# Loading four of sixteen input chunks of a Fourier stage by three wide transfers in place of eight narrower ones

## The chip, the cores and the metric

One core of one Trainium2 chip runs the whole program. The metric is device time in microseconds (us) of one execution, less is better. The kernel before took 1183.57 us, the median of three runs (1179.47 to 1185.5).

## What is computed

The input x has 2 batches of 3008 positions and 256 features. The reference is a Fourier layer followed by two wide two-layer networks:

```python
X = np.fft.rfft(x, axis=1)
Yr = Xr @ w_r - Xi @ w_i + b_r
Yi = Xr @ w_i + Xi @ w_r + b_i
Yr, Yi = shrink(Yr, 0.01), shrink(Yi, 0.01)   # sign(v) * max(|v| - lam, 0)
x = irfft(Y, n=3008)                          # 6016 rows of 256
h = x @ w_in;  x = (h * cos(h)) @ w_out       # 256 -> 2048 -> 256
h = x @ w_in2; x = (h * clip(h + 3, 0, 6) / 6) @ w_out2
```

## The kernel before, in words

The discrete Fourier transform over 3008 = 47 x 64 positions is cut in two. The first half, called part a here, multiplies slices of x by a table of sines and cosines ("ta"). Its work is listed in `a_list`: sixteen chunks, numbered 0 to 15, chunks 0 to 7 for batch 0 and 8 to 15 for batch 1. A chunk covers 4 of the 32 position pairs. Its x slice is 96 rows (partitions) of 4 pairs x 256 features x 4 bytes = 4 KB, 384 KB in all; its table slice is 96 rows of 4 x 96 x 4 bytes = 1.5 KB, 144 KB in all. Together a chunk is 528 KB.

`load_x` (line 494) issues a chunk's two transfers on SP's queue, the table first (line 504), then x (line 508; chunk 0's x goes in two pieces). Chunks 0 to 2 and 7 to 15 go through tiles "ta" and "x" with three buffers each. Chunks 3 to 6 have a place of their own, `x_big` (line 483): one persistent tile of 96 rows, in which each chunk has a stretch with 4 KB of x and then 1.5 KB of table. In HBM a row of x holds 32 KB for one batch, a row of the table 12 KB, so a chunk's rows are pieces of longer rows.

`a_part` (line 511) does half a chunk: four matrix products into one PSUM bank (line 515), a copy by ACT (line 524) and, for batch 0, a subtraction by DVE (line 526). In the loop of lines 718 to 729 the engine PE takes chunks 0 to 7 in order, two `a_part` calls each, and one dummy product (line 723, tile "wp") after each half. Nothing else is there for PE to do at that time. Only when chunk 7 is done can the next stage begin: `w_mm` (line 588, tile "pp") reads what all eight chunks wrote to zh and zl. Chunks 8 to 15 are then done one per step between the products of that stage.

The order on SP's queue is the order in which the code issues. Chunks 0 to 6 are issued ahead of everything (line 533), then the weights w_r and w_i of the layer (tile "wst", 256 KB each, lines 552 and 553), then chunk 7, the tables of the next stage (fg_raw, bias_raw), chunk 8 and so on. SP's transfers are counted on eight counters in turn (DMAHW0 to DMAHW7 in the rows of the order below), and a transfer that takes up a counter again first waits until the transfer eight before it has landed.

PE, SP and ACT run in the order in which the code is written here.

Of the kernel before, what the change touches and what calls it, by code (L numbers as in the profile page):

```python
# [9 lines left out]
F32 = mybir.dt.float32  # L10
# [11 lines left out]
NB, D, DFF = 2, 256, 2048  # L22
# [5 lines left out]
ROWS = 2 * DOF  # L28
# [22 lines left out]
XB, NBIG = 3, 4  # L51
# [73 lines left out]
def fourier_moe_moe_kernel(ctx, tc, x, w_r, w_i, b_r, b_i, ta, tg, fg, win1, wout1, win2, wout2, out):  # L125
    nc = tc.nc
    pe, act, dve, sp = nc.tensor, nc.scalar, nc.vector, nc.sync
# [4 lines left out]
    persist = ctx.enter_context(tc.tile_pool(name="persist", bufs=1))  # L132
# [343 lines left out]
    with ExitStack() as actx:  # L476
        apool = actx.enter_context(tc.tile_pool(name="apool", bufs=1))
        with tc.manual_schedule(engines={mybir.EngineType.PE, mybir.EngineType.SP, mybir.EngineType.Activation}):
# [1 line left out]
            zh = apool.tile([128, NP, 2, 4, N2], F32R, name="zh")  # L480
            zl = apool.tile([128, NP, 2, 4, N2], F32R, name="zl")

            x_big = persist.tile([ROWS, NBIG, 4 * (ROWS + D)], F32, tag="zt", name="x_big")
            z1 = None
            x_t, ta_t = {}, {}
            a_list = []
            for b in range(NB):
                p0 = 0
# [5 lines left out]
            def load_x(a):  # L494
                if a >= len(a_list):
                    return
                b, p0, n = a_list[a]
                if XB <= a < XB + NBIG:
                    tt = x_big[:, a - XB, 4 * D :]
                    xt = x_big[:, a - XB, : 4 * D].rearrange("p (n e) -> p n e", e=D)  # L500
                else:
                    tt = apool.tile([ROWS, 4 * ROWS], F32, tag="ta", bufs=XB, name=f"ta{a}")
                    xt = apool.tile([ROWS, 4, D], F32, tag="x", bufs=XB, name=f"x{a}")
                sp.dma_start(tt[:, : n * ROWS], ta[:, p0 * ROWS : (p0 + n) * ROWS])
                parts = 2 if a == 0 else 1
                for k in range(parts):
                    i0, i1 = k * n // parts, (k + 1) * n // parts
                    sp.dma_start(xt[:, i0:i1], x[b, :, p0 + i0 : p0 + i1, :])
                x_t[a], ta_t[a] = xt, tt
# [23 lines left out]
            for a in range(XB + NBIG):  # L533
                load_x(a)
# [131 lines left out]
            def k2_step(i):  # L666
# [28 lines left out]
                if a < 2 * NA:  # L695
                    a_part(a, 1)
                    load_x(a + XB)
# [20 lines left out]
            for c in range(NA):  # L718
                for kc in range(2):
                    if c == NA - 1:  # L720
                        constants(kc)
                    a_part(c, kc)
                    pe.matmul(wp, lhsT=warm[:, 0, 0:128], rhs=warm, start=True, stop=True)
                if c < XB:
                    load_x(XB + NBIG + c)
                if c == 0:
                    late_loads2()
                elif c == XB:
                    late_loads3()
# [27 lines left out]
    with tc.manual_schedule(engines=engines):  # L757
# [39 lines left out]
        def bank(z, name):  # L797
            return psum.tile([128, 512], F32, tag=f"h{z}", bufs=1, name=name)
# [123 lines left out]
        for k in range(2 * G):  # L922
            n = HALF[k // STEPS % NJ]
            a, b, c, d = (bank(z, f"h{r}_{k}") for z, r in zip((0, 1, 2, 3) if k % 2 == 0 else (0, 3, 2, 1), "abcd"))
# [125 lines left out]
```

## Time and profile before

| what | value |
|---|---|
| median of three runs | 1183.57 us (1179.47 to 1185.5) |
| the profiled execution's own time | 1183.19 us |
| its span (first to last instruction) | 1181.4 us |
| mean granted TensorE clock over the span | 0.998 |
| PE busy | 1157.2 us, 98% of the span |
| POOL, ACT, DVE busy | 67%, 69%, 64% |
| DMA | 101.98 MB, mean 86 GB/s |

PE has work almost all of the time, so a delay of PE early in the program is a delay of the end unless PE would have waited later anyway. The stage that the change touches lies in the first 30 us of the span. Times in the rows below count from the span's start. In the rows "SPq" is the transfer queue of SP; a row of it stands for the issue of a transfer, not for its landing.

### The profile page before, as it was taken

The page shows a single profiled execution, that of the slowest core. Times are in us where ns is not written, and L with a number is a line of the kernel's source. Part 1 is how long each engine was busy: PE and PEld are TensorE (multiplying, and loading weights), DVE is VectorE, ACT ScalarE, POOL GpSimd, SP SyncE. Part 2 cuts the span into 40 slices and gives each one's busy share as a digit, 9 for nine tenths or more (in the row PEclk, how much of TensorE's full clock was granted, in tenths as well). Part 3 has the DMA queues.
Part 4 walks back from the last instruction along what each step waited for, and adds up shares of the span by engine and source line. Part 5 has one row for each costly group of instructions (what it writes and reads, how often), then busy time and mean ns, then how long its engine had stood idle before and what let it go on. Part 6 is the DMA issues. An engine that isn't in the chain of part 4 may idle for free.

```text
span 1181.4 us, 15880 instructions
## 1 busy us (share of the span) xinstructions
PE 1157.2 (98%) x5379; PEld 967.7 (82%) x5379; DVE 760.5 (64%) x1090; ACT 812.1 (69%) x1542; POOL 795.8 (67%) x633
## 2 busy tenths in 40 slices
PE   8999898999999999999999999999999999999998
PEld 6888776778888888888888988888888888888897
DVE  3787768887679888898897677643343444433442
ACT  3677667777788888888888876665565556555554
POOL 0456455797778797888886886556757667667544
PEclk9999999999999999999999999999999999999999
DMA  9646647644431313103114520020020010100000
GB/s 229 173 124 181 200 150 249 231 118 128 134 109 57 90 60 116 54 19 132 52 36 152 197 103 1 1 72 1 1 72 1 12 61 1 60 8 1 36 1 32
DMA packets 49354, 101.98 MB, mean 86 GB/s; under 512 B 6164, under 2 KB 23832, under 8 KB 48632
## 3 DMA queue, kind: packets, MB, share of 16 engines
q1 hardware_dynamic: 49272, 100.97, 27.1%
q8 instruction: 42, 0.69, 0.3%
q14 instruction: 40, 0.33, 0.1%
HBM read 61.76 MB, written 39.19 MB: 85 GB/s over the span
## 4 chain that ended last, share of the span: by engine, by line
PE 88%; DMA 4%; DVE 3%; ACT 2%; POOL 1%; issue 1%; SPq 1%; POOLq 0%; DVEq 0%; ACTq 0%
PE acc L802 41%; PE hb L802 15%; PE ha L802 10%; PE hc L802 5%; PE hd L802 5%; PE pp L588 4%; PE yp L390 2%; PE bp L615 2%; PE zp L515 1%; DMA tg_sb<-in_tg_dram 1%; PE vp L654 1%; POOL gl L174 1%; DMA x_big<-in_x_dram 1%; DMA x<-in_x_dram 1%; DMA st<-x_dram 1%
## 5 line engine op out<-in xcount | busy, mean ns | idle before, releaser
L174 POOL TENSOR_TENSOR gl<-r,gh 128x512 fp32r<-128x512 f32 (+1 forms) x384 | 501.5, 1321 | 283.8 <-ACT gh L793 264.0
L802 PE MATMUL acc<-gh,wo 128*128 128x512 f32 (+1 forms) x1536 | 529.7, 386 | 0.0
L802 PEld LDWEIGHTS acc<-gh,wo 128*128 128x128 f32 x1536 | 288.4, 188 | 53.5
L802 PE MATMUL acc<-gl,wo 128*128 128x512 f32 (+1 forms) x768 | 295.9, 385 | 0.6 <-POOL gl L174 0.6
L802 PE MATMUL hb<-tok,wi 128*128 128x512 f32 (+1 forms) x864 | 241.0, 387 | 0.6 <-DVE hc L814 0.6
L793 ACT ACTIVATE gh<-r 128x512 fp32r<-128x512 f32 (+1 forms) x384 | 227.5, 615 | 0.4 <-PE acc L802 0.4
L802 PEld LDWEIGHTS hb<-tok,wi 128*128 128x128 f32 x864 | 160.9, 188 | 31.5 <-DVE hc L814 2.4
L814 DVE TENSOR_TENSOR hd<-p,hb 128x512 f32<-128x512 f32 (+1 forms) x96 | 65.7, 684 | 163.0 <-PE hb L802 157.9
L802 PEld LDWEIGHTS acc<-gl,wo 128*128 128x128 f32 x768 | 144.2, 188 | 27.6 <-POOL gl L174 1.0
L786 ACT ACTIVATE r<-r 128x512 f32<-128x512 f32 (+1 forms) x192 | 118.8, 619 | 62.5 <-DVE r L778 62.5
L802 PE MATMUL ha<-tok,wi 128*128 128x512 f32 (+1 forms) x576 | 160.2, 386 | 0.4 <-ACT yo L400 0.4
L802 PEld LDWEIGHTS ha<-tok,wi 128*128 128x128 f32 x576 | 107.8, 188 | 21.6 <-ACT yo L400 1.7
L439 POOL TENSOR_TENSOR tok<-st,tok 128x512 fp32r<-128x512 f32 (+1 forms) x77 | 97.6, 1282 | 4.1 <-ACT tok L436 4.1
L943 ACT ACTIVATE p<-hc 128x512 f32<-128x512 f32 (+1 forms) x96 | 56.6, 589 | 57.9 <-PE hc L802 57.8
L780 ACT ACTIVATE r<-hd 128x512 f32<-128x512 f32 (+1 forms) x48 | 28.3, 589 | 78.4 <-PE hd L802 78.4
L934 ACT ACTIVATE hb<-ha 128x512 f32<-128x512 f32 (+1 forms) x96 | 55.2, 575 | 38.5 <-PE ha L802 38.5
L802 PE MATMUL hc<-tok,wi 128*128 128x512 f32 (+1 forms) x288 | 80.2, 387 | 1.2 <-DVE r L787 1.1
L802 PE MATMUL hd<-tok,wi 128*128 128x512 f32 (+1 forms) x288 | 79.7, 385 | 0.0
L814 DVE TENSOR_TENSOR hc<-p,hb 128x512 f32<-128x512 f32 (+1 forms) x96 | 65.4, 681 | 15.2 <-PE hb L802 14.4
L802 PEld LDWEIGHTS hc<-tok,wi 128*128 128x128 f32 x288 | 53.7, 188 | 12.5 <-DVE r L787 2.6
L802 PEld LDWEIGHTS hd<-tok,wi 128*128 128x128 f32 x288 | 54.1, 188 | 10.1
L177 POOL TENSOR_TENSOR w<-cvai,cvbi 128x512 f32<-128x512 f32 x16 | 20.9, 1306 | 57.0 <-DVE cvbi L216 57.0
(134 smaller groups left out, 1709.0 us busy)
## 6 DMA issues: line engine op xcount, KB each, us to landing
st<-x_dram SPq DMA_DIRECT2D x20, 512.0 KB, 5.1
wi<-wi_dram SPq DMA_DIRECT2D x5, 1792.0 KB, 8.0
rawi<-in_win_dram SPq DMA_DIRECT2D x16, 512.0 KB, 4.2
rawo<-in_wout_dram SPq DMA_DIRECT2D x16, 512.0 KB, 4.0
u_dram<-v SPq DMA_DIRECT2D x48, 128.0 KB, 2.4
u_sb<-u_dram SPq DMA_DIRECT2D x16, 384.0 KB, 4.1
wo<-wo_dram SPq DMA_DIRECT2D x10, 512.0 KB, 7.6
x_dram<-o SPq DMA_DIRECT2D x20, 256.0 KB, 2.3
```

The lines of the kernel that those rows point to most:

```text
L174: nc.gpsimd.tensor_tensor(out, x, y, op=ALU.subtract)
L390: pe.matmul(yp[:, i * TP : (i + 1) * TP], lhsT=u_sb[g][:, i, ec * 128 : (ec + 1) * 128], rhs=tg_sb[g][:, i * TP : (i + 1) * TP], start=Tru ...
L439: subtract(at(lo, t), src, f32(at(hi, t)), op=ALU.subtract)
L588: pe.matmul(pp.rearrange("p a e -> p (a e)"), lhsT=za[:, p, kc, 2 * (k2 % 2) : 2 * (k2 % 2) + 2, :].rearrange("p r n -> p (r n)"), rhs=wb[ ...
L615: pe.matmul(bp, lhsT=fgr[:, fi, :], rhs=src[:, :, m, :], start=(n == 0 and not by_pe), stop=(n == 5))
L780: act.activation(r, h, AF.Relu, bias=3.0, scale=1.0)
L786: act.activation(r, r, AF.Sin, bias=math.pi / 2, scale=1.0)
L793: act.activation(gh[:, :n], self.r[:, :n], AF.Copy)
L802: pe.matmul(h[:, :n], lhsT=w, rhs=x, start=start and j == 0, stop=stop and j == 2, skip_group_check=True)
L814: dve.tensor_tensor(h[:, :n], r[:, :n], x[:, :n], op=ALU.add)
L934: act.activation(b[:, :n], a[:, :n], AF.Copy)
L943: act.activation(p5[:, :n], c[:, :n], AF.Copy)
```

## The change

The transfers of chunks 3 to 6 are replaced. The buffer `x_big` keeps its size and place, but is laid out as one stretch with the x of all four chunks (16 KB per row) and behind it the table of all four (6 KB per row). One transfer brings the whole table (96 rows of 6 KB, 576 KB), and two bring x, for two chunks each (96 rows of 8 KB, 768 KB). Chunks 3 to 6 read their pieces out of it.

```diff
-            x_big = persist.tile([ROWS, NBIG, 4 * (ROWS + D)], F32, tag="zt", name="x_big")
+            x_big = persist.tile([ROWS, NBIG * 4 * (ROWS + D)], F32, tag="zt", name="x_big")
+            big_x = x_big[:, : NBIG * 4 * D].rearrange("p (n e) -> p n e", e=D)
+            big_t = x_big[:, NBIG * 4 * D :]
...
                 if XB <= a < XB + NBIG:
-                    tt = x_big[:, a - XB, 4 * D :]
-                    xt = x_big[:, a - XB, : 4 * D].rearrange("p (n e) -> p n e", e=D)
+                    z = 4 * (a - XB)
+                    x_t[a], ta_t[a] = big_x[:, z : z + 4], big_t[:, z * ROWS : (z + 4) * ROWS]
+                    if z == 0:
+                        sp.dma_start(big_t, ta[:, p0 * ROWS : (p0 + 4 * NBIG) * ROWS])
+                    if z % 8 == 0:
+                        sp.dma_start(big_x[:, z : z + 8], x[b, :, p0 : p0 + 8, :])
+                    return
```

No instruction of PE, ACT, DVE or POOL is added, removed or moved. On SP's queue, before, chunks 3 to 6 and what follows (ta and x are the tiles of a chunk, the last number in a name counts buffers; the square brackets name the counters that the transfer waits for):

```order
L504 DMA x_big_108<-in_ta_dram 96x384
L508 DMA x_big_108<-in_x_dram 96x1024 [waits DMAHW0_49]
L504 DMA x_big_108<-in_ta_dram 96x384 [waits DMAHW1_49]
L508 DMA x_big_108<-in_x_dram 96x1024 [waits DMAHW2_49]
L504 DMA x_big_108<-in_ta_dram 96x384 [waits DMAHW3_49]
L508 DMA x_big_108<-in_x_dram 96x1024 [waits DMAHW4_49]
L504 DMA x_big_108<-in_ta_dram 96x384 [waits DMAHW5_49]
L508 DMA x_big_108<-in_x_dram 96x1024 [waits DMAHW6_49]
L552 DMA wst_148<-in_w_r_dram 128x2x256 [waits DMAHW7_49]
L553 DMA wst_148<-in_w_i_dram 128x2x256 [waits DMAHW0_49]
L504 DMA ta7_170<-in_ta_dram 96x384 [waits DMAHW1_49,PE_49]
L508 DMA x7_171<-in_x_dram 96x1024 [waits DMAHW2_49]
```

The same place in the changed kernel, whose line numbers are up to seven higher:

```order
L504 DMA x_big_108<-in_ta_dram 96x1536
L506 DMA x_big_108<-in_x_dram 96x2048 [waits DMAHW0_49]
L506 DMA x_big_108<-in_x_dram 96x2048 [waits DMAHW1_49]
L559 DMA wst_143<-in_w_r_dram 128x2x256 [waits DMAHW2_49]
L560 DMA wst_143<-in_w_i_dram 128x2x256 [waits DMAHW3_49]
L511 DMA ta7_165<-in_ta_dram 96x384 [waits DMAHW4_49,PE_49]
L515 DMA x7_166<-in_x_dram 96x1024 [waits DMAHW5_49]
```

Eight rows have become three, each of more bytes; the order of the rest is as it was, and each still waits for the transfer eight before it.

On PE, before, chunk 3 and the first product of chunk 4 (zp is the PSUM bank that they write, "warm" the dummy product's operand, x3 three more products alike):

```order
L515 MATMUL zp_0_219<-x_big 128x96 [waits DMAHW7_49,DMAHW0_49,DVE_49]
L515 MATMUL zp_0_219<-x_big 128x96 x3
L723 LDWEIGHTS warm
L723 MATMUL wp<-warm 128x512
L515 MATMUL zp_1_227<-x_big 128x96 [waits DVE_49]
L515 MATMUL zp_1_227<-x_big 128x96 x3
L723 LDWEIGHTS warm
L723 MATMUL wp<-warm 128x512
L515 MATMUL zp_0_243<-x_big 128x96 [waits DMAHW2_49,DMAHW1_49,DVE_49]
```

and in the changed kernel the end of chunk 3, chunk 4 and the first product of chunk 5:

```order
L522 MATMUL zp_1_222<-x_big 128x96 [waits DVE_49]
L522 MATMUL zp_1_222<-x_big 128x96 x3
L730 LDWEIGHTS warm
L730 MATMUL wp<-warm 128x512
L522 MATMUL zp_0_238<-x_big 128x96 [waits DVE_49]
L522 MATMUL zp_0_238<-x_big 128x96 x3
L730 LDWEIGHTS warm
L730 MATMUL wp<-warm 128x512
L522 MATMUL zp_1_246<-x_big 128x96 [waits DVE_49]
L522 MATMUL zp_1_246<-x_big 128x96 x3
L730 LDWEIGHTS warm
L730 MATMUL wp<-warm 128x512
```

The first product of chunk 4 (zp_0_238) has lost its wait for two transfers. Chunk 3's first product, ahead of these rows, still waits for two (DMAHW7 and DMAHW0), which are now the whole table and the x of two chunks; chunk 5's, behind them, waits for the second x transfer (DMAHW1).

## Rows read from the trace of the kernel before

**Rows 1.** The page: busy time of each engine.
```profile
PE 1157.2 (98%) x5379; PEld 967.7 (82%) x5379; DVE 760.5 (64%) x1090; ACT 812.1 (69%) x1542; POOL 795.8 (67%) x633
```
**Rows 2.** Chain of waits, 0 to 30 us: start us, us, what.
```profile
5.41 9.55 DMA x_big<-in_x_dram
...
14.97 8.98 DMA x<-in_x_dram
...
24.09 1.10 PE zp L515 x8
```
**Rows 3.** What PE waited for: total us, times, longest us.
```profile
PE zp L515 <- DMA x<-in_x_dram: 3.1, 2, 2.0
```
**Rows 4.** Timeline of PE: start us, us, engine line, tile [idle before].
```profile
8.30 1.10 PE L515 MATMUL zp<-ta,x 96*128 96x96 f32 x8 [1.11 <-DMA x<-in_x_dram]
...
12.59 0.38 PE L723 MATMUL wp<-warm 128*128 128x512 bf16 x1
12.80 1.10 PE L515 MATMUL zp<-x_big 96*128 96x96 f32 x8
13.74 0.38 PE L723 MATMUL wp<-warm 128*128 128x512 bf16 x1
13.96 1.03 PE L515 MATMUL zp<-x_big 96*128 96x96 f32 x8
...
19.72 1.10 PE L515 MATMUL zp<-x_big 96*128 96x96 f32 x8
...
24.09 1.10 PE L515 MATMUL zp<-ta,x 96*128 96x96 f32 x8 [1.96 <-DMA x<-in_x_dram]
...
25.30 1.86 PE L515 MATMUL zp<-ta,x 96*128 96x96 f32 x8
...
27.02 0.99 PE L588 MATMUL pp<-wh,zh 128*128 128x512 f32 x1
...
29.34 1.03 PE L515 MATMUL zp<-ta,x 96*128 96x96 f32 x8
30.15 0.48 PE L588 MATMUL pp<-wh,zh 128*128 128x512 f32 x1
...
31.62 1.03 PE L515 MATMUL zp<-ta,x 96*128 96x96 f32 x8
```
**Rows 5.** Timeline of SP: issues, each released by the landing eight before it.
```profile
8.18 0.31 SPq L508 DMA_DIRECT2D x_big<-in_x_dram  x1
...
10.44 0.31 SPq L508 DMA_DIRECT2D x_big<-in_x_dram  x1
...
12.72 0.39 SPq L553 DMA_DIRECT2D wst<-in_w_i_dram  x1
...
19.60 0.22 SPq L558 DMA_DIRECT2D bias_raw<-in_b_r_dram  x1
...
24.02 0.31 SPq L504 DMA_DIRECT2D ta<-in_ta_dram  x1
```
**Rows 6.** Stretches: busy us by engine, granted clock, DMA share, GB/s.
```profile
6.00:22.00 16.00, 14.89 (x118) 13.09 (x116) 7.25 (x13) 6.35 (x14) 0.00 (x0) 1.00 1.06 242
7.00:8.00 1.00, 0.19 (x1) 0.00 (x0) 0.47 (x2) 0.49 (x1) 0.00 (x0) 1.00 1.02 244
8.00:9.00 1.00, 0.70 (x6) 0.73 (x7) 0.09 (x1) 0.00 (x0) 0.00 (x0) 1.00 1.05 233
25.20:28.50 3.30, 3.30 (x13) 2.93 (x13) 1.99 (x4) 1.50 (x3) 0.00 (x0) 0.50 0.84 224
18.00:19.00 1.00, 1.00 (x11) 0.97 (x10) 0.40 (x1) 0.49 (x1) 0.00 (x0) 1.00 1.08 210
213.00:216.00 3.00, 3.00 (x15) 2.49 (x14) 2.96 (x3) 0.82 (x2) 2.67 (x2) 1.00 0.98 401
```
**Rows 7.** Transfers of the first 60 us by line: count, KB each, us to landing.
```profile
x_big<-in_x_dram SPq DMA_DIRECT2D x4, 384.0 KB, 8.9
```

## The prediction

> **What bounds the kernel now.** I read the page first: PE is busy 98% of the span [rows 1], so what counts is whatever makes PE idle or slow. The list of what PE waited for comes next. Of the waits for input, one line concerns the stage of the change: part a's products waited 3.1 us in all, twice, for an x transfer [rows 3]. The timeline of PE shows where: 1.11 us before chunk 1 (at 8.30) and 1.96 us before chunk 7 (at 24.09) [rows 4]. Between them chunks 1 to 6 follow each other without a wait; from the start of chunk 3 (12.80) to that of chunk 6 (19.72) a chunk takes (19.72 - 12.80) / 3 = 2.31 us [rows 4].
>
> The chain of waits says what stands behind chunk 7: two transfers, 9.55 and 8.98 us from issue to landing, fill the time from 5.41 to 23.95 [rows 2]; the four x transfers of chunks 3 to 6 take 8.9 in the median [rows 7]. These are long because they stand in line. The stretch from 6 to 22 us has a DMA share of 1.06 at 242 GB/s [rows 6]: all 16 engines always have something to move, and bytes set the pace. The timeline of SP gives the landings, since each issue there is released by the landing of the transfer eight before it: x of chunk 1 lands at 8.18, of chunk 2 at 10.44, of chunk 3 at 12.72, of chunk 6 at 19.60, of chunk 7 at 24.02 [rows 5]. Five chunks in 19.60 - 8.18 = 11.42 us is 2.28 us for a chunk's 528 KB. So data come at almost the rate at which PE uses them, chunk by chunk, and chunk 3 starts 0.08 us after its data are there.
>
> One more thing hangs on the last wait. [...] From chunk 7's start to the first product behind the six of line 588 it takes 29.34 - 24.09 = 5.25 us; at full clock a chunk takes 2.31 and the next such six, from 30.15 to 31.62, take 1.47 [rows 4], 3.78 together. The fall thus costs about 1.47 us. The 1.11 us of idleness before chunk 1 were not followed by a fall: the clock stays at 1.00 in the two stretches around it [rows 6].
>
> **The change part by part.** *Issues.* SP issues five transfers fewer, worth 0.31 us of its time each at the pace seen there [rows 5]. That is nothing for the sum: SP is waiting for landings anyway, and the engines behind it are never without work [rows 6].
>
> *Bytes.* They are the same, in the same places of the line up to chunk 2 and from wst on. If the rate holds, chunk 7 lands at 24.02 as before, and so does all that follows.
>
> *The rate.* No row of before shows 96 rows of 6 or 8 KB. The nearest row, and the one I take, is the same tensors in the same line at 242 GB/s (2.28 us per 528 KB). The upper end is 401 GB/s, in the stretch 213 to 216 us, which moves a weight tile of 128 rows of 14 KB; the lower is the slowest stretch in this line, 210 GB/s at 18 to 19 us [rows 6]. The first is far from this case in shape and source, so it stays an end. [...]
>
> *What chunk 3 waits for.* This is the cost. It needs the whole table (576 KB) and the x of two chunks (768 KB), 1344 KB behind chunk 2 instead of 528. At 2.28 us per 528 KB that is 5.81 us, so it can start at 10.44 + 5.81 + 0.08 = 16.33 instead of 12.80, and PE stands idle for 3.5 us more. Chunks 0 to 2 give no cover, and PE has no other work in that stage. At 401 GB/s the 1.376 MB take 3.43 us (start 13.95), at 210 GB/s 6.55 us (start 17.07).
>
> *What is late next.* The second x transfer lands 768 KB later, at 10.44 + 5.81 + 3.32 = 19.57; chunk 5 wants it at 16.33 + 2 x 2.31 = 20.95: no wait. Chunk 7 could start at 16.33 + 4 x 2.31 = 25.57, and its data are there at 24.02: the wait of 1.96 us is gone. Against 24.09 before, chunk 7 starts **1.48 us later**. The idle time has moved and grown.
>
> *The clock.* An idle time of 3.5 us is longer than the 1.96 us after which the clock fell, so I expect the fall behind chunk 3 instead of behind chunk 7, at the same price of 1.47 us: nothing for the sum. Bounds: nothing is lost, if the fall lies within the idle time (-1.47), or twice as much is (+1.47).
>
> *Behind chunk 7.* Products, copies and subtractions are the same, and chunk 8's data are in line as before. PE's next long wait for data is far off, so the delay reaches the end.
>
> Sum: +1.48 us against the profiled execution's 1183.19 us gives 1184.7; the median of the runs is 0.38 us above that execution, so **1185.0 us**. With the ends of clock and rate (210 GB/s: +0.74) the case spans 1183.6 to 1187.3.
>
> **The rivals.**
>
> *A, the forecast.* Its weak point is the clock. If the generator cuts wide rows into the old lengths, so that the change does not do what it says, the rate and therefore the time are A's.
>
> *B, wide rows move faster.* For it speaks that the same core moves 401 GB/s with 14 KB rows; against it that the line is slow by whole stretches, with rows of several lengths in it (210 to 244 GB/s) [rows 6]. At 401 GB/s for these three transfers chunk 3 starts at 13.95, after a wait about as long as the 1.11 us that left the clock alone. The second x transfer lands 0.786 MB later, at 15.83. What is ahead of chunk 7 then (512 KB of weights and 528 KB of its own, 1.065 MB) takes 4.40 us at 242 GB/s and lands at 20.2. Chunk 7 starts at 13.95 + 4 x 2.31 = 23.19, 0.90 us earlier, and the fall of 1.47 us is gone: -2.4 us, **1181.2 us**. [...]
>
> *C, the clock does not come back.* This is the side of slower. Before, the clock rose again while dense products of line 588 ran; behind chunk 3 there are only part a's short products and dummies for another five chunks. [...] With the late start of 1.48 us, and 0.85 us for the six products (29.34 - 27.02 = 2.32 at the low clock against 1.47), less the 1.47 us no longer lost, that is +6.5 to +12.5 us: **1190 to 1196 us**, middle 1193. Against it: the clock held at 1.00 from 6 to 22 us on this same work [rows 6]. It decides from about 6 us of loss to the clock on.
>
> **How the numbers follow.** A has 0.70, B 0.22, C 0.08. About 0.5%, 5.9 us here, is what a measurement of this kernel can tell from no change; the runs before spread over 6 us. A and B lie within it. C lies beyond it in most of its span: slower 0.06, and B with a lucky median gives faster 0.03, so 0.91 is left for no difference. The range is A's with its ends, down to B and up to where C begins: 1180.5 to 1189.
>
> **What would show it.** In the profile after: PE's wait for x_big before chunk 3, about 3.5 us, ending near 16.3, and no wait before chunk 7, which starts near 25.6; the DMA rate from 10 to 20 us near 240 GB/s; one stretch of clock 0.50 that starts behind chunk 3; the first product behind the six of line 588 (595 there) near 30.8 instead of 29.34. A start of chunk 3 before 14.5 and a rate over 300 GB/s would be B; a clock of 0.50 for more than 8 us would be C. The forecast is wrong if chunk 7 still waits for its data, or if the time leaves the range.

## The result, and the profile after

The changed kernel takes 1194.34 us, the median of four runs (1192.95 to 1198.73), against 1181.55 us for the kernel before, also of four (1179.47 to 1185.5). The ratio is 1.0098 with a 95% interval of 1.0075 to 1.0121: **slower by 1%**, and outside the range of the prediction, 1180.5 to 1189 us. The profiled executions, 1193.17 and 1183.19 us, differ by 10.0 us.

The page of the changed kernel, first line, then what PE waited for (total us, times, longest us).

```profile
PE 1165.8 (98%) x5377; PEld 976.4 (82%) x5379; DVE 761.4 (64%) x1090; ACT 812.8 (68%) x1542; POOL 796.4 (67%) x633
```
```profile
PE zp L522 <- DMA x_big<-in_x_dram: 3.1, 1, 3.1
...
PE zp L522 <- DMA x<-in_x_dram: 1.2, 1, 1.2
```

Beside [rows 1], PE is busy 8.6 us longer with the same instructions, and beside [rows 3] it waits for input 4.3 us instead of 3.1. So the waits are not where the 10 us are; PE is slower at its work. The granted clock says where. Stretches of the changed kernel (columns as in [rows 6]):

```profile
14.00:15.00 1.00, 0.00 (x0) 0.00 (x0) 0.00 (x0) 0.00 (x0) 0.00 (x0) 0.71 0.93 229
14.70:38.50 23.80, 22.53 (x94) 21.43 (x96) 7.42 (x13) 5.95 (x12) 0.00 (x0) 0.50 0.67 183
38.60:45.00 6.40, 6.40 (x42) 5.71 (x41) 2.49 (x4) 3.62 (x8) 0.00 (x0) 1.00 0.39 126
```

From 14.7 to 38.5 us the clock is 0.50, over all of chunks 3 to 7 and most of the six products behind them; before, it was so from 25.2 to 28.5 [rows 6]. It fell while PE was still idle: between 14 and 15 us, with PE busy for 0.00 us, the mean is 0.71. The timeline of PE (start us, us, engine line, tile [idle before]):

```profile
15.75 1.99 PE L522 MATMUL zp<-x_big 96*128 96x96 f32 x8 [3.09 <-DMA x_big<-in_x_dram]
...
32.52 1.86 PE L522 MATMUL zp<-ta,x 96*128 96x96 f32 x8
...
38.83 1.03 PE L522 MATMUL zp<-ta,x 96*128 96x96 f32 x8
```

Held against [rows 4], the 10 us add up. Chunk 3 starts at 15.75 instead of 12.80. Four chunks take 32.52 - 15.75 = 16.77 us, 4.19 each instead of 2.31. So chunk 7 starts at 32.52 instead of 24.09: 8.43 us late. Without the clock it would have started at 15.75 + 4 x 2.31 = 24.99, so 0.90 us of this are the data's and 7.53 the clock's. From chunk 7 to the first product behind the six of line 595 it takes 6.31 us instead of 5.25, 1.06 more. That product stands at 38.83 instead of 29.34, **9.49 us late**; the spans differ by 10.0 us, so the rest of the program adds about half a microsecond.

The landings, read from SP's issues as in [rows 5]:

```profile
10.07 0.35 SPq L563 DMA_DIRECT2D fg_raw<-in_fg_dram  x1
...
15.68 0.22 SPq L565 DMA_DIRECT2D bias_raw<-in_b_i_dram  x1
19.32 0.22 SPq L565 DMA_DIRECT2D bias_raw<-in_b_r_dram  x1
...
23.72 0.31 SPq L511 DMA_DIRECT2D ta<-in_ta_dram  x1
```

Chunk 2's x lands at 10.07, the first wide x at 15.68, the second at 19.32 and chunk 7's x at 23.72. So the 2112 KB of chunks 3 to 6 take 9.25 us, where the eight narrow transfers took 19.60 - 10.44 = 9.16. The wide rows move no faster.

### The profile page after: what moved, and what is told of

The parts are those of the page before. It is cut to its first block, busy times and chain, and to the rows that moved or that the text cites. A ratio compares the mean times of both kernels' runs of the same rounds, so it can differ in the third digit from the quotient of the medians.

```text
span 1191.4 us, 15870 instructions
## 1 busy us (share of the span) xinstructions
PE 1165.8 (98%) x5377; PEld 976.4 (82%) x5379; DVE 761.4 (64%) x1090; ACT 812.8 (68%) x1542; POOL 796.4 (67%) x633
## 4 chain that ended last, share of the span: by engine, by line
PE 84%; issue 4%; POOL 3%; DVE 3%; DMA 3%; ACT 2%; SPq 1%; POOLq 0%; DVEq 0%; ACTq 0%
PE acc L809 38%; PE hb L809 14%; PE ha L809 10%; PE hc L809 5%; PE hd L809 5%; PE pp L595 4%; POOL gl L174 3%; PE zp L522 3%; PE yp L390 2%; PE bp L622 2%; DMA tg_sb<-in_tg_dram 1%; DMA x_big<-in_x_dram 1%; PE vp L661 1%; DMA st<-x_dram 1%; ACT r L793 0%
## 5 line engine op out<-in xcount | busy, mean ns | idle before, releaser
L809 PEld LDWEIGHTS hc<-tok,wi 128*128 128x128 f32 x288 | 53.7, 188 | 12.5 <-DVE r L794 2.5
```

Source lines behind the costliest of these rows:

```text
L809: pe.matmul(h[:, :n], lhsT=w, rhs=x, start=start and j == 0, stop=stop and j == 2, skip_group_check=True)
```

## The experiments

The theory after reading the result: PE's long idle time before chunk 3 makes the clock fall, and part a's short products, which had held it at 1.00 from 6 to 22 us [rows 6], do not bring it back; only the next stage does. The rivals: the wide transfers themselves harm (their rows, or what they do to the data's order), or the late data cost the time without the clock.

### No idle time: dummies before chunk 3

To the changed kernel, in the loop over the chunks:

```diff
+                if c == 2:
+                    for _ in range(15):
+                        pe.matmul(wp, lhsT=warm[:, 0, 0:128], rhs=warm, start=True, stop=True)
                 if c < XB:
                     load_x(XB + NBIG + c)
```

> The changed kernel, and on PE 15 dummy products more between chunk 2 and chunk 3, into the same unused bank as the others (15 x 0.21 us = 3.2 us, the length of the idle time there). Theory: the loss is the clock's, which falls because PE is idle before chunk 3 and does not come back on part a's short products. Then chunk 3 starts near 15.8 as in the changed kernel, but at full clock; chunk 7 starts near 15.8 + 9.2 = 25.0, the first product behind the six of line 595 near 28.8 (38.83 in the changed kernel), and the time is some 10 us lower, 1183 to 1186. Rival: the loss is the late data themselves or something that the wide transfers do to PE's reads; then the time stays above 1190.

Measured: 1182.72 us, median of ten, against 1184.27 us for the kernel before on the same chip; ratio 0.9981 (0.9966 to 0.9997). Timeline of PE and a stretch:

```profile
16.91 1.10 PE L522 MATMUL zp<-x_big 96*128 96x96 f32 x8 [0.38 <-issue]
...
25.67 2.11 PE L522 MATMUL zp<-ta,x 96*128 96x96 f32 x16
...
29.32 1.03 PE L522 MATMUL zp<-ta,x 96*128 96x96 f32 x8
```
```profile
16.90:29.00 12.10, 11.97 (x94) 11.41 (x96) 6.74 (x13) 5.95 (x12) 0.00 (x0) 1.00 0.97 235
```

("issue" in a row means that the profile shows no releaser; the SP row that tells the landing stands at 16.84 here.) Chunk 3 starts even later than in the changed kernel, at 16.91, but at full clock, and chunk 7 starts at 25.67. Same transfers, data at least as late, 15 products more, and the loss against the kernel before is gone: the first product behind the six stands at 29.32, before it stood at 29.34. That rules out both rivals as the cause of the 10 us. It does not show that the late data cost nothing. Chunk 7 starts 1.58 us later than before, and what makes up for it is that the fall behind chunk 7, which the kernel before pays for, is gone too: from chunk 7 to that product it takes 3.65 us instead of 5.25.

### Narrow rows, the same bytes ahead of chunk 3

To the kernel before:

```diff
-            for a in range(XB + NBIG):
+            for a in range(XB):
                 load_x(a)
+            for a in range(XB, XB + NBIG):
+                b, p0, n = a_list[a]
+                x_t[a] = x_big[:, a - XB, : 4 * D].rearrange("p (n e) -> p n e", e=D)
+                ta_t[a] = x_big[:, a - XB, 4 * D :]
+                sp.dma_start(ta_t[a], ta[:, p0 * ROWS : (p0 + n) * ROWS])
+            for a in (XB + 1, XB, XB + 3, XB + 2):
+                b, p0, n = a_list[a]
+                sp.dma_start(x_t[a], x[b, :, p0 : p0 + n, :])
```

> The kernel before, with its eight narrow transfers (rows of 1.5 and 4 KB), but issued so that chunk 3 waits for the same 1344 KB: the four tables first, then x of chunk 4, 3, 6, 5. Theory: the row length does nothing, the bytes ahead of chunk 3 do all; chunk 3 starts between 15.7 and 16.5, the clock falls and stays low for over 20 us, and the time is that of the changed kernel, 1191 to 1199. Rival: wide rows are what is bad; then the time is near that of before, 1181 to 1185.

Measured: 1194.17 us, median of four, ratio 1.0068 (1.0047 to 1.0090). Timeline of PE and a stretch:

```profile
15.58 2.00 PE L515 MATMUL zp<-x_big 96*128 96x96 f32 x8 [2.98 <-issue]
...
32.35 1.86 PE L515 MATMUL zp<-ta,x 96*128 96x96 f32 x8
```
```profile
15.60:39.40 23.80, 23.58 (x98) 22.23 (x100) 7.41 (x13) 6.03 (x13) 0.00 (x0) 0.50 0.69 185
```

With eight narrow transfers in this order the kernel is as slow as with three wide ones, as far as four runs each can tell (the intervals of the two ratios overlap). Chunk 3 starts at 15.58, right behind the landing of its x at 15.55, the clock stays at 0.50 for 23.8 us, and four chunks take 32.35 - 15.58 = 16.77 us, the same as in the changed kernel. So the loss does not need wide rows; what counts is that 1344 KB instead of 528 stand ahead of chunk 3.

### More dummies behind each half, the idle time left as it is

To the changed kernel:

```diff
                     a_part(c, kc)
-                    pe.matmul(wp, lhsT=warm[:, 0, 0:128], rhs=warm, start=True, stop=True)
+                    for _ in range(4 if c >= XB else 1):
+                        pe.matmul(wp, lhsT=warm[:, 0, 0:128], rhs=warm, start=True, stop=True)
```

> The changed kernel, idle time left as it is, with four dummy products in place of one behind each half of chunks 3 to 7. [...]

Measured: one run, 1190.68 us. Timeline of PE and two stretches:

```profile
16.72 1.99 PE L522 MATMUL zp<-x_big 96*128 96x96 f32 x8 [3.85 <-DMA x_big<-in_x_dram]
...
38.22 1.03 PE L522 MATMUL zp<-ta,x 96*128 96x96 f32 x8
```
```profile
15.90:22.60 6.70, 5.88 (x23) 4.58 (x24) 0.56 (x1) 0.98 (x2) 0.00 (x0) 0.52 1.03 255
22.70:38.00 15.30, 15.19 (x103) 11.91 (x103) 6.79 (x12) 4.96 (x10) 0.00 (x0) 1.00 0.58 164
```

PE waits 3.85 us before chunk 3, the clock falls, and with three dummies more per half it is back from 22.7 us on, at the end of chunk 3, long before the next stage. The first product behind the six stands at 38.22. At 0.50 throughout, as an estimate, a chunk would take the 4.19 us of the changed kernel and six more dummies of 0.43 (four took from 18.50 to 20.21 here), five chunks thus 33.9 us from 16.72 on, and that product would stand beyond 50. So in this execution the clock waited neither for the next stage nor for the 23.8 us that it took in the changed kernel; with other work on PE it came back earlier. From chunk 3's start to that product it takes 21.50 us, in the changed kernel 23.08: the 30 dummies cost most of what the earlier return saves, so this is a proof and no remedy.

### Wide x, narrow tables: a shorter wait

To the changed kernel:

```diff
-                    if z == 0:
-                        sp.dma_start(big_t, ta[:, p0 * ROWS : (p0 + 4 * NBIG) * ROWS])
+                    sp.dma_start(ta_t[a], ta[:, p0 * ROWS : (p0 + 4) * ROWS])
                     if z % 8 == 0:
```

> The changed kernel with the table of chunks 3 to 6 in four narrow transfers again, each just ahead of its x; x stays in two wide ones. Chunk 3 then waits for 912 KB behind chunk 2: 10.1 + 912/528 x 2.2 = 13.9, an idle time of 1.3 us, between the 1.15 that the clock took without falling and the 1.96 that made it fall in the kernel before. Theory: the loss comes from the length of that idle time; the clock holds, chunk 7 starts near 23.8 and the time is 1179 to 1183. Rival: wide x transfers cost the time wherever the table stands; then over 1190.

Measured: median 1184.46 us of ten runs, ratio 1.0013 (0.9986 to 1.0039), but the runs fall into two groups: six of 1181.74 to 1185.27 us, with a mean granted clock of 0.997 to 1.000, and four of 1189.93 to 1192.25 us with 0.990 or 0.991. The profiled one, 1191.67 us, is of the second group. Timeline of PE and a stretch:

```profile
14.90 1.10 PE L521 MATMUL zp<-x_big 96*128 96x96 f32 x8 [1.57 <-DVE zl L532]
```
```profile
16.40:36.80 20.40, 20.18 (x85) 19.07 (x86) 7.41 (x13) 5.59 (x12) 0.00 (x0) 0.51 0.82 206
```

(The row names DVE as the releaser, a copy long done; the first product of chunk 3 waits for DVE and for two transfers, and it is the transfers that were late: by SP's issues chunk 3's x landed at 14.83.) By the mean clock, my expectation that it holds was right for six runs in ten and wrong for four. An idle time of 1.57 us was enough in the profiled run, and the price is nearly that of 3.09 us, some 9 us between the two groups: once down, the clock stayed down for the rest of part a (0.51 from 16.4 to 36.8 us).

### The kernel before without its own fall

Two ways to remove the wait of 1.96 us before chunk 7 [rows 4] from the kernel before. First, dummies in it:

```diff
+                if c == 6:
+                    for _ in range(9):
+                        pe.matmul(wp, lhsT=warm[:, 0, 0:128], rhs=warm, start=True, stop=True)
                 if c < XB:
                     load_x(XB + NBIG + c)
```

> The kernel before, and on PE nine dummy products more between chunk 6 and chunk 7 (9 x 0.21 us = 1.9 us, the idle time there). Theory: the kernel before pays for the same thing in small, 1.47 us for a fall behind chunk 7; without the fall the first product behind the six of line 588 starts near 24.1 + 3.8 = 27.9 instead of 29.34, and the time is 1 to 1.5 us lower than before in those runs in which the clock fell. Rival: the fall behind chunk 7 costs nothing, since that stage waits for the copies of ACT and DVE; then no difference.

Measured: 1181.76 us against 1184.21, ratio 0.9971 (0.9957 to 0.9985). Timeline of PE and a stretch:

```profile
23.35 1.03 PE L515 MATMUL zp<-ta,x 96*128 96x96 f32 x8
...
27.01 1.03 PE L515 MATMUL zp<-ta,x 96*128 96x96 f32 x8
```
```profile
21.00:30.00 9.00, 9.00 (x59) 7.14 (x58) 4.50 (x8) 4.11 (x8) 0.00 (x0) 1.00 0.92 246
```

From chunk 7 to the first product behind the six it takes 27.01 - 23.35 = 3.66 us instead of 5.25, so the fall cost 1.59 us there, against the 1.47 of the prediction. The medians differ by 2.45 us, more than the 1 to 1.5 expected. The granted clock of the runs says why in part. Of the 71 runs of the kernel before that were taken beside the experiments, 25 have a mean clock of 0.995 or less, and their median is 1186.33 us; the 16 runs with 0.998 or more have 1183.04, and the profiled execution, with 0.998, is one of that kind. So the kernel before often loses more to the clock than its trace shows. With nine dummies, in this series and the one repeated below, 1 run of 24 has 0.995 or less.

Second, a cause of the wait moved: the weights w_r and w_i (512 KB) behind chunk 7 in the line.

```diff
-            late_loads()
             for c in range(NA):
                 for kc in range(2):
-                    if c == NA - 1:
-                        constants(kc)
                     a_part(c, kc)
...
                 if c == 0:
+                    late_loads()
                     late_loads2()
...
+            constants(0)
+            constants(1)
             z1 = persist.tile([128, NP, 2, 4, N2], F32, tag="zt", name="z1")
```

> The kernel before, with the two weight transfers (512 KB) issued behind chunk 7's transfers, not ahead of them, and their conversion behind chunk 7's halves. Chunk 7 then lands near 24.0 - 512/528 x 2.28 = 21.8 and PE does not wait; it waits instead for the weights after chunk 7, from 24.3 to 25.4 or so, on the first products of the next stage. Theory: the idle time shrinks from 1.96 to about 1 us, the clock does not fall, and the first product behind the six starts near 27.0 instead of 29.34: 2 us lower than before, 1182. Rival: the late weights with their conversions on ACT and DVE take the place of the wait; then no difference.

Measured: 1182.48 us, ratio 0.9981 (0.9968 to 0.9994). Timeline of PE:

```profile
25.36 0.49 PE L588 MATMUL pp<-wh,zh 128*128 128x512 f32 x1 [0.88 <-ACT wh L568]
...
27.35 1.03 PE L515 MATMUL zp<-ta,x 96*128 96x96 f32 x8
```

The wait has become two short ones for the converted weights, 0.88 and 0.23 us, the clock did not fall in this execution (1.00 from 22 to 30 us), and the first product behind the six stands at 27.35, close to the 27.0 expected.

### Combinations

The changed kernel with the 15 dummies and the later weights, both edits as above:

> The changed kernel with both, the 15 dummy products before chunk 3 and the weights behind chunk 7's transfers. Theory: chunk 7 is bound by PE there, not by data (chunk 3 starts near 16, chunk 7 near 25), so putting the weights later brings nothing over the 15 dummies alone: 1182 to 1184. Rival: it was the weights in the line that held chunk 7; then some 2 us below that.

Measured: 1183.95 us, ratio 0.9999 (0.9984 to 1.0014). Chunk 7 starts at 25.12, bound by PE, and PE then waits 0.88 us for the weights. As the theory had it, the weights were not what held chunk 7 there. One of the twelve runs took 1191.33 us at a mean clock of 0.993; it was not profiled.

The kernel before with the later weights and, behind chunk 7, four dummies:

```diff
+                if c == 7:
+                    for _ in range(4):
+                        pe.matmul(wp, lhsT=warm[:, 0, 0:128], rhs=warm, start=True, stop=True)
```

> The kernel before with the weights behind chunk 7's transfers (as in the earlier run) and four dummy products (0.85 us) in the 0.88 us that PE then waits for the converted weights. Theory: in that version the clock no longer fell with the short wait alone, so the dummies cover nothing that costs; the time is the same as without them, 2 us below before (1182 against 1184). Rival: the short wait still makes the clock fall in some runs; then the median is a further 1 us lower and the slower runs are gone.

> The kernel before with nine dummy products before chunk 7, once more, beside the other version: 0.3% below before, about 1181.5 to 1182 against 1184. If the weights behind chunk 7 are worth something beyond the clock, this one is slower than its neighbour by about 1 us; if the clock was all, the two are equal.

Measured together: 1181.29 us, ratio 0.9983 (0.9958 to 1.0008), for the first, one of its twelve runs at 1195.76 (with a mean clock of 0.999, so what made it long is not the clock, and is not known); 1181.36 us, ratio 0.9972 (0.9957 to 0.9988), for the second. The two are equal within what twelve runs can tell, so the later weights bring no more than the nine dummies do. Whether the four dummies gain anything over the later weights alone stays open: the two ratios, 0.9983 and 0.9981, were taken in different series, and their intervals overlap. The kernel before with nine dummies beats both kernels: it is 0.3% below the one before in two series, and so, by the two ratios, 1.3% below the changed one.

## Why the prediction was wrong

The steps on the data held. Chunk 3 was to start at 16.33 and did at 15.75; in the three other executions with the same transfers ahead of it, it did at 16.4 to 16.9. The second x was to land at 19.57 and did at 19.32, chunk 7's x at 24.02 and did at 23.72. The bytes took the time that they took before, 9.25 us against 9.16; rival B, faster wide rows, fell with that. Putting eight transfers of 144 and 384 KB that already stand in line together into three brought nothing here. The second x transfer held nothing up, and the wait before chunk 7 was gone, in the run with 15 dummies also at full clock. Without the clock, chunk 7 would have been 0.90 us late, 1.48 were forecast.

**The step that failed** is "The clock": "I expect the fall behind chunk 3 instead of behind chunk 7, at the same price of 1.47 us: nothing for the sum". The fall that it takes the price from is that of the granted clock to 0.50, from 25.2 to 28.5 us [rows 6]. In the changed kernel the fall came with the wait before chunk 3, as expected. It even came within the idle time, for which the prediction's lower bound had put its price at nothing. The price was 7.53 us on chunks 3 to 6 and 2.53 more from chunk 7 on (6.31 us against the 3.78 at full clock), 10.06 in all. I took the price from a fall that was followed, half a chunk later, by the dense products of the next stage, and moved it to a place where five chunks of short products come first. The run with 15 dummies shows that without the fall nothing of the loss is left but the late data's 0.9 to 1.6 us, and the run with four dummies per half that PE's own work has a part in when the low clock ends: it was back at 1.00 from 22.7 us on there, from 38.6 in the changed kernel.

It was rival C. Its span of +6.5 to +12.5 us holds 5.6 to 11.6 us for five chunks at the low clock. Half a chunk takes 13.96 - 12.80 = 1.16 us at a granted clock of 1.00 and 27.02 - 25.30 = 1.72 at 0.50 [rows 4, 6], so ten halves lose 5.6 us, and 5 x 2.31 = 11.6 if all doubles. That brackets what five chunks lost: 5 x (4.19 - 2.31) = 9.4 us, if chunk 7 is put like the four ahead of it. The middle of the span, 1193, is 1.3 us from the median, but that is in part luck. The lower price takes 1.72 us for half a chunk at 0.50, and this half is cut short: the next stage's first product starts beside its dummy. A whole half took 2.08 us (from 17.96 to 20.04 in the changed kernel), so a price of 5.6 us was never to be had, while the 1.48 us put down for the late start were too much. What I got wrong was its chance, 0.08, and the argument for it: "the clock held at 1.00 from 6 to 22 us on this same work". That showed that part a's work kept a high clock, not that it brings one back. It held 1.00 for the 16 us from 6 to 22 before the change [rows 6] and did not restore it in the 20 us of chunks 3 to 7 after it; the clock was back at 1.00 from 38.6 us on, after the first products of line 595.

The sum was also made at one point where it should have been a fork: a step with two outcomes, of 1.5 and of some 10 us, deserved two forecasts of comparable weight, and a range that reached to 1196.

What stays open: what exactly in the four dummies brought the clock back (their number, their length or their type), and why the clock stayed low in four runs of ten only with the narrow tables. The wait is known for one of those ten, the profiled one (1.57 us); whether it was shorter in the six others, no trace shows. Neither was tried.

## What to carry to other kernels

The first user of a larger transfer waited here for its last byte: chunk 3, which needs half of the first wide x, started at 15.75 us, behind the landing of all its 768 KB at 15.68. Where transfers stood in line, merging them left the rate as it was (9.25 us for 2112 KB against 9.16) and only moved the first start back, from 12.80 to 15.75: ask what the first consumer needs, not how many transfers there are. An idle time of PE can cost more than its length: here 3.09 us of it were followed by 23.8 us at a granted clock of 0.50, which cost 10.06 us, so look at what comes behind the gap. A few dummy products in the gap were cheap insurance here: nine of them brought 0.3%.

## What was not expected of the hardware

The price of a fallen clock hardly depended on the gap that caused it. Gaps of 1.57, 2.98 and 3.09 us ahead of chunk 3 were each followed by 20 us or more at 0.50 or 0.51, the gap of 1.96 us ahead of chunk 7 by 3.3 us at 0.50 [rows 6], and the gap of 3.85 us in the run with four dummies per half by 6.7 us at 0.52. What differs between these is the work behind the gap. And wider rows were no faster in this line. By SP's issues the 2112 KB of chunks 3 to 6 took 9.25 us with three wide transfers (rows of 6 and 8 KB) in the changed kernel, 9.10 in the run with 15 dummies and 9.50 in the one with four per half, and 9.16 us with eight narrow ones (rows of 1.5 and 4 KB) in the kernel before.
